# The last output tile of an SSM and SwiGLU kernel: its down projection placed later, and the tile in two column parts

## The chip, the cores and the metric

The kernel runs on one core of a Trainium2 chip. The metric is device time in microseconds (us) of one execution, and each kernel is run several times. A profile is taken of one execution. Every execution also has a span, from its first to its last instruction; in the kernel before it is about 1.8 us less than the device time. Engines are TensorE (PE, its weight loads PEld), VectorE (DVE), ScalarE (ACT), GpSimd (POOL) and the sync engine (SP), which issues most transfers. A name with a q at its end (DVEq, SPq, ACTq) stands for an instruction of that engine's sequencer, such as a semaphore wait or the issue of a transfer; "issue" alone is time in which the engine waited for nothing that the profile shows. The landing of a store is the time from its issue until it is reported as done. A PSUM bank is a piece of the memory that matmuls write to.

## The reference

```python
x  = A_x                                   # (1, 2048, 448) bf16
xn = layernorm(x)
s  = ssm(xn)                               # linear recurrence over 2048 tokens, 448 complex states
g  = silu((silu(xn @ w_gate) * (xn @ w_up)) @ w_down)     # inner width 1792
out = x + s * g                            # (1, 2048, 448) bf16
```

## The kernel before

The 2048 tokens go in four groups of 512, each with four tiles of 128 tokens. For a tile, `down` does the down projection (14 matmuls of 448 columns into one PSUM bank) and ScalarE makes the gate `sg` of it. `out_sum` does the state's output (7 matmuls of 448 columns with `C2`, and 4 small ones that add the skip term), and `finish` multiplies by the gate, adds x and stores. The code is shortened; `...` stands for what is left out.

```python
def down(q, j):
    hd = bank("hd")[:, 0:D]
    for fi in range(NF):                                   # 14
        nc.tensor.matmul(hd, lhsT=Vt_of[q][:, fi, j*P:(j+1)*P], rhs=Wd[:, fi, :], ...)
    sg = work.tile([P, D], BF16, name="sg", bufs=TQ)
    nc.scalar.activation(sg[:], hd, ACT.Silu)
    return sg

def out_sum(q, j):
    y = bank("y")[:, 0:D]
    for n in range(NS):                                    # 7
        h = H_of[q][n // KT][:, n % KT, j*P:(j+1)*P]
        nc.tensor.matmul(y, lhsT=h, rhs=C2[:, n, :], ...)
        if n < KT:                                         # 4: skip term, 128 columns (the last 64)
            ...
    return y

def finish(q, j, y, sg):
    m = q * TQ + j
    t = work.tile([P, D], F32, name="t", bufs=1)
    nc.vector.tensor_tensor(out=t[:], in0=y, in1=sg[:], op=ALU.mult)
    ob = work.tile([P, D], BF16, name="ob")                # two buffers
    nc.vector.tensor_tensor(out=ob[:], in0=t[:], in1=x_all[:, m, :], op=ALU.add)
    nc.sync.dma_start(out=out2d[m*P:(m+1)*P, :], in_=ob[:])

# ... the end of the kernel, the last group of tokens:
q = NQ - 1
bg.finish(q)
sg = [down(q, j) for j in range(TQ)]
for j in range(TQ):
    finish(q, j, out_sum(q, j), sg[j])
```

The instructions stand on each engine in the order in which the program records them.

Of the kernel before, what the change touches and what calls it, by code (L numbers as in the profile page):

```python
# [10 lines left out]
ALU = mybir.AluOpType  # L11
ACT = mybir.ActivationFunctionType
BF16 = mybir.dt.bfloat16
F32 = mybir.dt.float32
# [7 lines left out]
class Background:  # L22
# [16 lines left out]
    def finish(self, owner):  # L39
        while any(step[0] == owner for step in self.steps):  # L40
            self.steps.popleft()[2]()
# [3 lines left out]
def kernel(  # L45
# [17 lines left out]
    nc = tc.nc  # L63
    P = nc.NUM_PARTITIONS
    _, L, D = A_x.shape
    F = B_w_gate.shape[1]
    W = 512
    KF = D // P
    R = D - KF * P
    KT = KF + 1  # L70
    NQ = L // W
    TQ = W // P
    NT = L // P
    NF = F // P
    NS = 2 * KF + 1
# [13 lines left out]
    def blk(k):  # L89
        return slice(k * P, k * P + P) if k < KF else slice(D - P, D)  # L90
# [8 lines left out]
    out2d = out[0]  # L99
# [3 lines left out]
    work = ctx.enter_context(tc.tile_pool(name="work", bufs=2))  # L103
# [3 lines left out]
    def ctile(shape, dtype, name):  # L107
        return const.tile(shape, dtype, name=name)

    def bank(name, dtype=F32):  # L110

        return psum.tile([P, 2048 // mybir.dt.size(dtype)], dtype, name=name, tag="bank")
# [5 lines left out]
    x_all = ctile([P, NT, D], BF16, "x_all")  # L118
    xT = ctile([P, KT, L], BF16, "xT")
# [4 lines left out]
    C2 = ctile([P, NS, D], BF16, "C2")  # L124
    Dd = ctile([P, KT, P], BF16, "Dd")
# [56 lines left out]
    for n in range(2):  # L182
# [11 lines left out]
        out=Id[:], in_=Id[:], compare_op=ALU.not_equal, fill=1.0,  # L194
# [368 lines left out]
    def down(q, j):  # L563

        hd = bank("hd")[:, 0:D]
        for fi in range(NF):
            nc.tensor.matmul(  # L567
                hd, lhsT=Vt_of[q][:, fi, j * P : (j + 1) * P], rhs=Wd[:, fi, :],
                start=(fi == 0), stop=(fi == NF - 1),
            )  # L570
        sg = work.tile([P, D], BF16, name="sg", bufs=TQ)
        nc.scalar.activation(sg[:], hd, ACT.Silu)  # L572
        return sg

    def out_sum(q, j):

        y = bank("y")[:, 0:D]
        m = q * TQ + j
        for n in range(NS):
            h = H_of[q][n // KT][:, n % KT, j * P : (j + 1) * P]  # L580
            nc.tensor.matmul(y, lhsT=h, rhs=C2[:, n, :], start=(n == 0), stop=(n == NS - 1))  # L581
            if n < KT:
                c0 = 0 if n < KF else P - R
                s = blk(n).start
                nc.tensor.matmul(  # L585
                    y[:, s + c0 : s + P], lhsT=xT[:, n, m * P : (m + 1) * P],
                    rhs=Dd[:, n, c0:P], start=False, stop=False,
                )
        return y

    def finish(q, j, y, sg):
        m = q * TQ + j
        t = work.tile([P, D], F32, name="t", bufs=1)
        nc.vector.tensor_tensor(out=t[:], in0=y, in1=sg[:], op=ALU.mult)  # L594
        ob = work.tile([P, D], BF16, name="ob")
        nc.vector.tensor_tensor(out=ob[:], in0=t[:], in1=x_all[:, m, :], op=ALU.add)  # L596
        nc.sync.dma_start(out=out2d[m * P : (m + 1) * P, :], in_=ob[:])


    bg = Background()  # L600
# [82 lines left out]
    for q in range(NQ - 1):  # L683
        sg = []
        for j in range(TQ):
            sg.append(down(q, j))
            bg.run(2.2)
# [3 lines that stand above are left out]
        if q + 2 < NQ:  # L691
            drive(q + 2, "first", 4.0)
            n = (q + 3) * TQ
            last = q + 3 == NQ
            gu(q + 2, bg, 2.2 if last else 1.5, {} if last else {
                0: stats(n, n + 1),
                1: stats(n + 2, n + 3) + sqrt(q + 3),
                2: rstd_of(q + 3) + norms(n, n + 1),
                3: norms(n + 2, n + 3) + transposes(n, n + 1),
                4: transposes(n + 2, n + 3),  # L700
            })
    q = NQ - 1
    bg.finish(q)
    sg = [down(q, j) for j in range(TQ)]
    for j in range(TQ):
        finish(q, j, out_sum(q, j), sg[j])

# [1 line left out]
_INS = ['A_x', 'A_Lambda_re', 'A_Lambda_im', 'A_B_re', 'A_B_im', 'A_C_re', 'A_C_im', 'A_log_dt', 'A_Dskip', 'B_x', 'B_w_gate', 'B_w_up', 'B_w_down']  # L709
_OUTS = [((1, 2048, 448), 'bfloat16')]  # L710
# [25 lines left out]
```

## Time and profile before

| | before |
|---|---|
| device time, median of 3 runs (lowest to highest) | 190.68 us (190.6 to 190.87) |
| span of the profiled execution | 188.8 us |
| TensorE busy | 182.8 us (97%) |
| VectorE busy | 160.0 us (85%) |
| last group: first down projection starts | 167.85 us |
| last matmul's columns are all in ("end of the stream") | 184.53 us |
| last ob ends / last store lands / span ends | 186.07 / 187.8 / 188.8 us |

TensorE is busy from end to end, so the interest lies in the last row: 4.3 us in which it does nothing. The start of the last group stands in the timeline (start us, us, engine, line, what, count):

```profile
167.85 10.76 PE L567 MATMUL hd<-Wd,Vt 128*128 128x448 bf16 x56
```

The 56 are four down projections of 14 matmuls in one run. The end of the stream is the start of the last three matmuls, 183.96, plus three times their spacing of 0.189.

### The profile page before, as it was taken

The page shows a single profiled execution, that of the slowest core. Times are in us where ns is not written, and L with a number is a line of the kernel's source. Part 1 is how long each engine was busy: PE and PEld are TensorE (multiplying, and loading weights), DVE is VectorE, ACT ScalarE, POOL GpSimd, SP SyncE. Part 2 cuts the span into 40 slices and gives each one's busy share as a digit, 9 for nine tenths or more (in the row PEclk, how much of TensorE's full clock was granted, in tenths as well). Part 3 has the DMA queues.
Part 4 walks back from the last instruction along what each step waited for, and adds up shares of the span by engine and source line. Part 5 has one row for each costly group of instructions (what it writes and reads, how often), then busy time and mean ns, then how long its engine had stood idle before and what let it go on. Part 6 is the DMA issues. An engine that isn't in the chain of part 4 may idle for free.

```text
span 188.8 us, 3686 instructions
## 1 busy us (share of the span) xinstructions
PE 182.8 (97%) x1465; PEld 92.5 (49%) x1465; DVE 160.0 (85%) x265; ACT 104.0 (55%) x197; POOL 10.9 (6%) x21
## 2 busy tenths in 40 slices
PE   7899999999999999999999999999999999999991
PEld 3575435555555455544444455544444455555550
DVE  4889995999999999989999899789259999888073
ACT  3288599939998862008987722107987542302200
POOL 6423100000110000000020000000000000000000
PEclk9999999999999999999999999999999999999999
DMA  5999999100012100021006000020000000020011
GB/s 160 343 380 384 377 144 203 28 0 2 0 31 56 31 0 0 0 72 32 0 5 103 6 0 3 24 73 0 3 2 0 3 0 0 0 76 24 0 38 61
DMA packets 20977, 12.59 MB, mean 67 GB/s; under 512 B 10976, under 2 KB 19936, under 8 KB 20960
## 3 DMA queue, kind: packets, MB, share of 16 engines
q1 hardware_dynamic: 20288, 12.10, 24.5%
q10 hardware_dynamic: 544, 0.26, 0.5%
q8 instruction: 11, 0.18, 0.4%
q14 instruction: 6, 0.05, 0.1%
q0 software_dynamic: 128, 0.00, 0.0%
HBM read 8.03 MB, written 1.84 MB: 52 GB/s over the span
## 4 chain that ended last, share of the span: by engine, by line
PE 94%; DVE 2%; DMA 1%; ACT 0%; POOL 0%; issue 0%; DVEq 0%
PE gp L428 24%; PE hd L567 23%; PE up L428 21%; PE y L581 11%; PE pb L428 10%; PE pk L453 2%; PE y L585 2%; DMA x_all<-in_A_x_dram 1%; PE tpb L371 1%; DVE st L230 1%; PE tp L259 1%; DVE t L594 0%; DVE ob L596 0%; ACT xT L261 0%; POOL sd L215 0%; DVE xn L248 0%
## 5 line engine op out<-in xcount | busy, mean ns | idle before, releaser
L428 PE MATMUL gp<-xT,Wg 64*128 64x512 bf16 (+1 forms) x406 | 86.2, 369 | 0.1
L428 PE MATMUL up<-xT,Wu 64*128 64x512 bf16 (+1 forms) x406 | 85.9, 369 | 0.0
L428 PEld LDWEIGHTS <-Wg 64*128 64x128 bf16 x406 | 37.1, 94 | 23.8 <-issue 1.6
L428 PEld LDWEIGHTS <-Wu 64*128 64x128 bf16 x406 | 37.3, 94 | 19.4 <-POOLq L410 0.3
L567 PE MATMUL hd<-Wd,Vt 128*128 128x448 bf16 x224 | 43.0, 353 | 0.0
L554 ACT ACTIVATE gs<-gp 128x512 bf16<-128x512 f32 x56 | 35.0, 626 | 10.9 <-PE gp L428 7.4
L555 ACT ACTIVATE us<-up 128x512 bf16<-128x512 f32 x56 | 35.4, 632 | 0.0
L567 PEld LDWEIGHTS <-Vt 128*128 128x128 bf16 x224 | 21.8, 98 | 21.0 <-issue 0.8
L572 ACT ACTIVATE sg<-hd 128x448 bf16<-128x448 f32 x16 | 8.7, 544 | 33.7 <-PE hd L567 33.7
L559 DVE TENSOR_TENSOR Vt<-gs,us 128x2048 bf16<-128x2048 bf16 (+1 forms) x16 | 17.3, 1082 | 6.3 <-ACT us L555 6.3
L428 PE MATMUL pb<-xT,BT 64*128 64x512 bf16 x168 | 19.2, 376 | 0.0
L594 DVE TENSOR_TENSOR t<-y,sg 128x448 f32<-128x448 f32 x16 | 10.0, 623 | 10.6 <-PE y L581 10.2
L466 ACT ACTIVATE bu_re<-pb 128x512 bf16<-128x512 f32 x12 | 7.3, 609 | 20.9 <-PE pb L428 20.9
L581 PE MATMUL y<-C,H_re 128*128 128x448 bf16 x64 | 17.4, 352 | 0.0
L504 DVE TENSOR_TENSOR_SCAN bu_re<-rcol,H_re,ere 128x512 bf16<-128x512 f32 x12 | 15.1, 1269 | 0.0
L585 PE MATMUL y<-Dd,xT 128*128 128x128 bf16 x64 | 13.6, 212 | 0.0
L428 PEld LDWEIGHTS <-BT 64*128 64x128 bf16 x168 | 8.4, 94 | 10.0 <-issue 1.3
L581 PE MATMUL y<-C,H_im 128*128 128x448 bf16 x48 | 11.7, 353 | 0.0
L504 DVE TENSOR_TENSOR_SCAN bu_im<-rcol,H_im,eim 128x512 bf16<-128x512 f32 x9 | 11.3, 1260 | 0.0
L230 DVE BATCH_NORM_STATS2 st<-x_all 128x6 f32<-128x448 bf16 x16 | 9.8, 615 | 1.5 <-DMA x_all<-in_A_x_dram 1.5
L596 DVE TENSOR_TENSOR ob<-t,x_all 128x448 bf16<-128x448 f32 x16 | 10.0, 625 | 0.5
L215 POOL TENSOR_TENSOR sd<-vep,halves 128x1 bf16<-128x1 bf16 (+1 forms) x7 | 5.7, 814 | 77.2 <-PE up L428 41.8
(95 smaller groups left out, 174.4 us busy)
## 6 DMA issues: line engine op xcount, KB each, us to landing
out_dram<-ob SPq DMA_DIRECT2D x16, 112.0 KB, 1.7
Wd<-in_B_w_down_dram SPq DMA_DIRECT2D x1, 1568.0 KB, 11.8
x_all<-in_A_x_dram SPq DMA_DIRECT2D x1, 896.0 KB, 13.7
Wg<-in_B_w_gate_dram SPq DMA_DIRECT2D x1, 768.0 KB, 7.0
Wu<-in_B_w_up_dram SPq DMA_DIRECT2D x1, 768.0 KB, 8.5
x_all<-in_A_x_dram SPq DMA_DIRECT2D x1, 448.0 KB, 5.2
Wg<-in_B_w_gate_dram SPq DMA_DIRECT2D x1, 384.0 KB, 5.1
Wu<-in_B_w_up_dram SPq DMA_DIRECT2D x1, 384.0 KB, 5.5
```

Of the source, the lines that this page charges most:

```text
L230: nc.vector.bn_stats(out=st[:], in_=x_all[:, n, :])
L428: mm = nc.tensor.matmul(banks[n][i][:, c0:c1], lhsT=weights[n][i][h, d, :], rhs=xT[h, d, q * W + c0 : q * W + c1], start=(first and m == 0 ...
L504: nc.vector.tensor_tensor_scan(out=T["b"][c][:, k, :], data0=rcol[:, k : k + 1].to_broadcast([P, W]), data1=T["e"][c][:, k, :], initial=in ...
L554: nc.scalar.activation(gs[:, i + j, :], gp_[:], ACT.Silu)
L555: nc.scalar.activation(us[:, i + j, :], up_[:], ACT.Copy)
L559: nc.vector.tensor_tensor(out=Vt[:, f0 : f0 + n, :], in0=gs[:, 0:n, :], in1=us[:, 0:n, :], op=ALU.mult)
L567: nc.tensor.matmul(hd, lhsT=Vt_of[q][:, fi, j * P : (j + 1) * P], rhs=Wd[:, fi, :], start=(fi == 0), stop=(fi == NF - 1),)
L572: nc.scalar.activation(sg[:], hd, ACT.Silu)
L581: nc.tensor.matmul(y, lhsT=h, rhs=C2[:, n, :], start=(n == 0), stop=(n == NS - 1))
L585: nc.tensor.matmul(y[:, s + c0 : s + P], lhsT=xT[:, n, m * P : (m + 1) * P], rhs=Dd[:, n, c0:P], start=False, stop=False,)
L594: nc.vector.tensor_tensor(out=t[:], in0=y, in1=sg[:], op=ALU.mult)
L596: nc.vector.tensor_tensor(out=ob[:], in0=t[:], in1=x_all[:, m, :], op=ALU.add)
```

## The change

The intent: shorten what follows the last matmul. The down projection of the last tile goes between the last two output tiles, so that the third tile's VectorE work is over when the last tile comes. The last tile is made in two column parts (256 and 192 columns) with their own PSUM banks, their own buffers (the tags `scr_f` and `scr_a`: scratch of the kernel's beginning, two buffers each) and two queues, so that part one's VectorE work can lie beside part two's matmuls. The diff is shortened.

```diff
-    def out_sum(q, j):
-        y = bank("y")[:, 0:D]
+    def out_sum(q, j, k0=0, k1=KT):
+        y = bank("y")
+        c0, c1 = k0 * P, min(k1 * P, D)
         for n in range(NS):
-            nc.tensor.matmul(y, lhsT=h, rhs=C2[:, n, :], ...)
-            if n < KT:
+            nc.tensor.matmul(y[:, c0:c1], lhsT=h, rhs=C2[:, n, c0:c1], ...)
+            if k0 <= n < k1:
                 ...
-        return y
+        return y[:, c0:c1]

-    def finish(q, j, y, sg):
+    def finish(q, j, y, sg, eng=nc.sync, c0=0, c1=D):
-        t = work.tile([P, D], F32, name="t", bufs=1)
+        of = dict(tag="scr_f") if c1 - c0 < D else dict(bufs=1)
+        t = work.tile([P, c1 - c0], F32, name="t", **of)
         ...
-        ob = work.tile([P, D], BF16, name="ob")
+        of = dict(tag="scr_a") if c1 - c0 < D else {}
+        ob = work.tile([P, c1 - c0], BF16, name="ob", **of)
         ...
-        nc.sync.dma_start(out=out2d[m * P : (m + 1) * P, :], in_=ob[:])
+        eng.dma_start(out=out2d[m * P : (m + 1) * P, c0:c1], in_=ob[:])

-    q = NQ - 1
+    q, last = NQ - 1, TQ - 1
     bg.finish(q)
-    sg = [down(q, j) for j in range(TQ)]
-    for j in range(TQ):
+    sg = [down(q, j) for j in range(last)]
+    for j in range(last):
         finish(q, j, out_sum(q, j), sg[j])
+    sg = down(q, last)
+    for k0, k1, eng in ((0, 2, nc.sync), (2, KT, nc.scalar)):
+        finish(q, last, out_sum(q, last, k0, k1), sg, eng, k0 * P, min(k1 * P, D))
```

More of the change, by code (lines that the diff above doesn't have):

```diff
@@ L573, in down @@
         return sg
-    def out_sum(q, j):
-        y = bank("y")[:, 0:D]
+    def out_sum(q, j, k0=0, k1=KT):
+        y = bank("y")
         m = q * TQ + j
+        c0, c1 = k0 * P, min(k1 * P, D)
         for n in range(NS):
             h = H_of[q][n // KT][:, n % KT, j * P : (j + 1) * P]
-            nc.tensor.matmul(y, lhsT=h, rhs=C2[:, n, :], start=(n == 0), stop=(n == NS - 1))
-            if n < KT:
-                c0 = 0 if n < KF else P - R
+            nc.tensor.matmul(
+                y[:, c0:c1], lhsT=h, rhs=C2[:, n, c0:c1], start=(n == 0), stop=(n == NS - 1)
+            )
+            if k0 <= n < k1:
+                skip = 0 if n < KF else P - R
                 s = blk(n).start
                 nc.tensor.matmul(
-                    y[:, s + c0 : s + P], lhsT=xT[:, n, m * P : (m + 1) * P],
-                    rhs=Dd[:, n, c0:P], start=False, stop=False,
-                )
-        return y
-    def finish(q, j, y, sg):
+                    y[:, s + skip : s + P], lhsT=xT[:, n, m * P : (m + 1) * P],
+                    rhs=Dd[:, n, skip:P], start=False, stop=False,
+                )
+        return y[:, c0:c1]
+    def finish(q, j, y, sg, eng=nc.sync, c0=0, c1=D):
         m = q * TQ + j
-        t = work.tile([P, D], F32, name="t", bufs=1)
-        nc.vector.tensor_tensor(out=t[:], in0=y, in1=sg[:], op=ALU.mult)
-        ob = work.tile([P, D], BF16, name="ob")
-        nc.vector.tensor_tensor(out=ob[:], in0=t[:], in1=x_all[:, m, :], op=ALU.add)
-        nc.sync.dma_start(out=out2d[m * P : (m + 1) * P, :], in_=ob[:])
+        of = dict(tag="scr_f") if c1 - c0 < D else dict(bufs=1)
+        t = work.tile([P, c1 - c0], F32, name="t", **of)
+        nc.vector.tensor_tensor(out=t[:], in0=y, in1=sg[:, c0:c1], op=ALU.mult)
+        of = dict(tag="scr_a") if c1 - c0 < D else {}
+        ob = work.tile([P, c1 - c0], BF16, name="ob", **of)
+        nc.vector.tensor_tensor(out=ob[:], in0=t[:], in1=x_all[:, m, c0:c1], op=ALU.add)
+        eng.dma_start(out=out2d[m * P : (m + 1) * P, c0:c1], in_=ob[:])
     bg = Background()
```

## The prediction

> **What bounds the kernel now.** I read the chain that ended last first, because it says which engine sets the end. The summary of the page gives TensorE (PE) 94% of the span:
>
> ```profile
> PE 94%; DVE 2%; DMA 1%; ACT 0%; POOL 0%; issue 0%; DVEq 0%
> ```
>
> TensorE streams almost without a gap from the first microseconds to 184.5 us, and the change removes no product there. So nearly all of the 188.8 us cannot move; what can is the short stretch after the last matmul. I therefore read the chain again in its last microseconds (start us, us, what):
>
> ```profile
> 184.13 0.58 PE y L581 x3
> 184.71 0.04 DVEq L594
> 184.74 0.04 issue
> 184.79 0.64 DVE t L594
> 185.43 0.02 issue
> 185.45 0.62 DVE ob L596
> ```
>
> The last output tile ends on TensorE, VectorE multiplies it by the gate (t), then adds x (ob), and only then is the result stored. The store's own row, restricted to the last issue, and the program's end (line 731, from the same trace) complete the tail:
>
> ```profile
> L597 SPq DMA_DIRECT2D out_dram<-ob x1: 332/332/332, 186.1 to 186.1; - x1
> DMA to landing us min/median/max: 1.7/1.7/1.7
> ...
> L731 SPq DRAIN  x3: 7/7/13, 188.0 to 188.3; - x3
> ```
>
> So the tail reads: TensorE's stream ends near 184.53 us; t starts at 184.79; ob ends at 185.45 + 0.62 = 186.07; the store is issued at 186.1, lands 1.7 later at about 187.8; about 1.0 us of closing semaphores follows to 188.8. Of these 4.3 us after the stream, only the two VectorE instructions (1.28 us with their gap) are work whose size the change touches; the store's flight and the close are waits. The timeline around the three earlier tiles shows that their VectorE work lies under TensorE's next tile:
>
> ```profile
> 178.65 0.54 ACT L572 ACTIVATE sg<-hd 128x448 bf16<-128x448 f32 x1 [2.10 <-PE hd L567]
> ...
> 181.75 0.62 DVE L594 TENSOR_TENSOR t<-y,sg 128x448 f32<-128x448 f32 x1 [0.23 <-PE y L581]
> ...
> 182.41 0.62 DVE L596 TENSOR_TENSOR ob<-t,x_all 128x448 bf16<-128x448 f32 x1
> ```
>
> VectorE needs 1.28 us for a tile and TensorE 1.52, so VectorE sits idle some 0.23 us before each t.
>
> **What the Trainium skill says, and whether this trace agrees.** "VectorE: DVE Perf Modes", section on the TRN2 errata, gives an fp32 tensor_tensor of N columns (N+151)/0.96 ns. For 448 columns that is 624 ns; the trace has 623 (t) and 625 (ob), and 692 ns for 512 columns where the formula says 691. It agrees, so I use it for the new widths: 256 columns 424 ns, 192 columns 357 ns.
>
> "TensorE: Matmul & The Clock Gate", section "Wait — 56ns, not 53.3ns?", puts back-to-back warm matmuls N/2.4 + about 2.5 ns apart. One output tile is seven of 448 columns, three of 128 and one of 64: 7 x 189.2 + 3 x 55.8 + 29.2 = 1521 ns. In the trace successive tiles start at 178.45, 179.97, 181.49 and 183.01, 1.52 us apart. It agrees.
>
> "DMA: Bandwidth & Descriptors", section "Anatomy of one DMA", says that the fixed part of about 2 us is mostly the wait for the write receipt; its "Specifications" add that pieces under 512 B are below line rate because of a read-modify-write. Here all 16 stores of 112 KB in rows of 896 B have a median landing of 1.7 us. A row of 192 bf16 columns is 384 B, and no store of that row length exists in this trace, so its landing is not settled by it. The same page, "Issuing engines are not separate DMA queues", says a second issuing engine saves only sequencer time; on the before trace the issue on the sync queue costs 0.33 us and is never waited for by the next store.
>
> **The change, part by part.**
>
> *Order.* The fourth down projection (14 matmuls of 448 columns, 14 x 189.2 = 2.65 us) moves from before the first output tile to between the third and the last. TensorE's work is the same. The first output tile then starts 2.65 us sooner, at about 175.8 instead of 178.45. It needs the last H_re, whose VectorE instruction starts at 172.57 and takes 1.23, so it is ready at 173.80: 2.0 us to spare, no stall. What it buys: the third tile's t and ob (0.26 + 1.28 us after its stream) are done under the 2.65 us of down projection, so VectorE is free when the last tile's first part comes. Its own gate has to come in time. The last down projection's stream ends at 183.01 (worked out below); sg starts 0.20 after that as it does now (178.65 against 178.45) and takes 0.54, so it is ready at 183.75. I compare that with the first t below.
>
> *Split on TensorE.* Part one has seven matmuls of 256 columns and two of 128: 7 x 109.2 + 2 x 55.8 = 876 ns. Part two has seven of 192, one of 128 and one of 64: 7 x 82.5 + 55.8 + 29.2 = 662 ns. Sum 1538 against 1521: 7 more matmuls, 0.017 us more. TensorE's stream ends at 184.53 + 0.02 = 184.55; part one at 184.55 - 0.66 = 183.89, and so the last down projection at 183.89 - 0.88 = 183.01. The waits compiled in for the new banks are on events of several microseconds before.
>
> *Split on VectorE.* From the end of a tile's stream to t is 0.26 us now (184.53 to 184.79). So t of part one starts at 183.89 + 0.26 = 184.15, after sg's 183.75; it ends at 184.57. ob of part one runs 184.61 to 185.03, with the same gap of 0.03 to 0.04 between dependent instructions. t of part two could start at 184.55 + 0.26 = 184.81, but VectorE is still in ob. An instruction that does not depend on ob starts before ob's recorded end: at 168.77 + 0.63 = 169.40 an ob ends, and the next instruction has begun at 169.31. So t of part two starts at about 185.03 - 0.09 = 184.94, ends 185.30; ob of part two runs 185.33 to 185.69. Before, ob ended at 186.07. **This is the gain: 0.38 us.** The same from the other side: 1.28 + 0.26 = 1.54 us lay after the stream; now it is 0.26 + 0.13 (waiting for VectorE) + 0.36 + 0.03 + 0.36 = 1.14, less 0.02 for the longer stream.
>
> *Stores.* Part one (64 KB, rows of 512 B) is issued on the sync queue at about 185.06 and lands near 186.8, out of the way. Part two (48 KB) goes out on ScalarE's queue, idle since sg. Its 48 KB instead of 112 KB is at most 0.15 us less by the skill's 436 GB/s (an estimate from that page); the short rows and a queue unused since 1.7 us pull the other way. I set the sum to zero and put it into the range: landing 1.7 after 185.72, at 187.4. The close follows as before.
>
> Span 188.8 - 0.38 = 188.4; time 190.68 - 0.38 = **190.3 us**, 0.2% less.
>
> **The rivals.**
>
> First: the last store eats the gain. 384 B rows are under 512 B, and the two stores are in flight together from 185.72 to 186.8. For it: the page's line on short pieces; both run on the same engines. Against: eight short rows for each of 16 engines are little beside a flight that is mostly receipt, and the first store's data should have moved before the second's starts. If the landing took 0.3 us longer, the time would be 190.6.
>
> Second: short matmuls become bound by the weight loads. Each load is listed with 98 ns, more than the 82.5 ns spacing of part two. Were that the spacing, part two would be some 7 x 15 = 0.11 us longer, and since VectorE is busy for 0.13 us of that anyway nothing much would be seen at the end (190.3 still). Against it: the trace already has whole 128-row loads at a shorter spacing:
>
> ```profile
> 9.70 1.06 PE L371 MATMUL tpb<-Id,nat 128*128 128x128 bf16 x16
> ```
>
> Sixteen in 1.06 us, a load each: (1.06 - 0.22) / 15 = 0.056 us apart.
>
> Third: the order hurts: TensorE waits for H_re, or the first t waits for sg. The margins above, 2.0 and 0.4 us, speak against it; a wait of 0.3 for sg would pass on only in part, giving 190.5.
>
> Fourth: the store lands sooner, being smaller, by up to 0.15 us: 190.15.
>
> **Range and chances.** The VectorE sum is from measured durations and good to about 0.1 us. The landing is good to 0.2 us in either direction. The three runs before spread over 0.27 us (190.6 to 190.87), so a median can be off by 0.1. Together about 0.25 to each side, a little more to the slow side for the store: 190.05 to 190.65. A change of 2% would be 3.8 us; the whole tail is 4.3 us and no new wait of that size is in sight, so within 2% is near certain.
>
> **What would show it right or wrong.** In the profile after: the first output tile on TensorE at about 175.8 with no gap before it; y to y spacing of 0.109 and 0.082 us for the new widths; t and ob of 424 and 357 ns; t of part two beginning about 0.4 us after TensorE's stream ends, held by VectorE and not by TensorE; last ob near 185.7; last issue on ScalarE's queue, landing 1.7 us later; span 188.4. I am wrong if the last landing takes clearly more or less than 1.7 us, if the first t waits for ScalarE, or if TensorE's stream ends more than 0.1 us from 184.55.

## The result, and the profile after

The changed kernel took 190.31 us (median of 4 runs, 190.14 to 190.72) against 190.64 for the kernel before (4 runs, 190.6 to 190.87). A ratio here is the mean time of one kernel's fast runs over that of the other's, so not quite the ratio of the medians. It was 0.9983, with an interval of 0.9965 to 1.0001. Two later sets of five and six runs gave 190.15 and 190.20, with ratios of 0.9973 and 0.9976 (told below).

The first thing to see in the profile after is that its span is 188.9 us, longer than before. This one execution was the slowest of its four, at 190.72. The timelines of VectorE near the beginning show why. The first fence is before, the second after (in brackets: idle time before the instruction, and what ended it):

```profile
3.77 0.62 DVE L230 BATCH_NORM_STATS2 st<-x_all 128x6 f32<-128x448 bf16 x1
```

```profile
4.38 0.63 DVE L230 BATCH_NORM_STATS2 st<-x_all 128x6 f32<-128x448 bf16 x1 [0.48 <-DMA x_all<-in_A_x_dram]
...
168.46 8.11 PE L567 MATMUL hd<-Wd,Vt 128*128 128x448 bf16 x42
```

The second tile of x landed late in that execution, its statistics began 0.61 us later, and the last group began 0.61 us later too (168.46 against 167.85). The change touches nothing there. The two delays go together in other profiles too: of the thirteen profiles besides that of before, eleven have the same delay against it, to 0.02 us, at these statistics and at the last group (e4's and e8's groups lost another 0.17 and 0.22 in between). A span read without this would say that nothing was gained. From the start of the last group, the tail of the timeline after reads so:

```profile
173.17 1.22 DVE L498 TENSOR_TENSOR H_re<-H_re,tmp 128x2048 bf16<-128x2048 bf16 x1
...
176.22 0.10 PEld L582 LDWEIGHTS <-H_re 128*128 128x128 bf16 x1
...
183.62 0.27 PE L582 MATMUL y<-C,H_re 128*128 128x256 bf16 x1
...
183.82 0.54 ACT L572 ACTIVATE sg<-hd 128x448 bf16<-128x448 f32 x1 [6.67 <-PE hd L567]
...
184.91 0.41 PE L582 MATMUL y<-C,H_im 128*128 128x192 bf16 x3
```

H_re is ready at 174.39, 1.8 us before the first output tile's first weight load (176.22) and 2.0 before its first matmul (176.41), so the new order costs TensorE nothing. Part one starts on TensorE at 183.62. The gate is ready at 184.36. The last stream ends at 184.91 + 3 x 0.0825 = 185.16, which is 16.70 us after the group's start; before it was 16.68. The chain of waits then shows what lies after the stream (start us, us, what):

```profile
184.70 0.02 DVEq L598
184.72 0.04 issue
184.76 0.43 DVE t L598
185.20 0.02 issue
185.22 0.42 DVE ob L601
185.65 0.28 DVE t L598
185.92 0.02 issue
185.95 0.36 DVE ob L601
```

Four VectorE instructions stand in a row where there were two, but the first two lie beside part two's matmuls. The second t is on the chain behind ob of part one, and not behind a matmul: VectorE held it. (The chain cuts the overlap of neighbours; the timeline has this t starting at 185.56.) The last ob ends at 186.31, 17.85 us after the group's start, against 18.22 before. The last store:

```profile
L602 ACTq DMA_DIRECT2D out_dram<-ob x1: 353/353/353, 186.3 to 186.3; - x1
...
DMA to landing us min/median/max: 1.5/1.5/1.6
```

It landed 1.5 us after its issue instead of 1.7. From the group's start the span ends at 20.4 us, before at 20.95: some 0.5 us gained, of which 0.37 is VectorE's and about 0.2 the store's, each rounded. A little of it is lost again outside the span: device time exceeds the span by 1.82 to 1.88 us in the four executions of the changed kernel (spans are known to 0.1), by about 1.79 in the mean of the kernel before.

### The profile page after: what moved, and what is told of

It reads as the page before. It is cut to its first block, busy times and chain, and to the rows that moved or that the text cites. A ratio compares the mean times of both kernels' runs of the same rounds, so it can differ in the third digit from the quotient of the medians.

```text
span 188.9 us, 3703 instructions
## 1 busy us (share of the span) xinstructions
PE 182.9 (97%) x1472; PEld 93.0 (49%) x1472; DVE 160.3 (85%) x267; ACT 104.0 (55%) x197; POOL 10.9 (6%) x21
## 4 chain that ended last, share of the span: by engine, by line
PE 94%; DMA 2%; DVE 2%; ACT 0%; POOL 0%; issue 0%; SPq 0%; DVEq 0%
PE gp L428 24%; PE hd L567 23%; PE up L428 21%; PE y L582 11%; PE pb L428 10%; PE pk L453 2%; DMA x_all<-in_A_x_dram 2%; PE y L588 2%; PE tpb L371 1%; PE tp L259 1%; DVE ob L601 0%; DVE t L598 0%; DVE st L230 0%; ACT xT L261 0%; POOL sd L215 0%
## 5 line engine op out<-in xcount | busy, mean ns | idle before, releaser
L598 DVE TENSOR_TENSOR t<-y,sg 128x448 f32<-128x448 f32 (+2 forms) x17 | 10.1, 595 | 10.0 <-PE y L582 9.6
L582 PE MATMUL y<-C,H_re 128*128 128x448 bf16 (+2 forms) x68 | 17.6, 342 | 0.0
L582 PE MATMUL y<-C,H_im 128*128 128x448 bf16 (+2 forms) x51 | 11.9, 342 | 0.0
L601 DVE TENSOR_TENSOR ob<-t,x_all 128x448 bf16<-128x448 f32 (+2 forms) x17 | 10.2, 597 | 0.6
```

Source lines behind the costliest of these rows:

```text
L582: nc.tensor.matmul(y[:, c0:c1], lhsT=h, rhs=C2[:, n, c0:c1], start=(n == 0), stop=(n == NS - 1))
L598: nc.vector.tensor_tensor(out=t[:], in0=y, in1=sg[:, c0:c1], op=ALU.mult)
```

## The experiments

Twelve runs were made. The kernel before was measured beside them, but not anew for each: e1 to e4 share its 11 executions, e5 to e8 share 9, and e9 to e12 are compared with the same 9 and one more. "ob" and "span" are the ends of the last ob and of the span, counted from the start of the last group; spans are known to 0.1.

| run | ob | span | last store: KB, landing | device time: median (lowest to highest) | ratio to before (interval) |
|---|---|---|---|---|---|
| before | 18.22 | 20.95 | 112, 1.7 | 190.65 beside e1 to e4, 190.81 and 190.80 beside the others | |
| e1_again | 17.84 | 20.4 | 48, 1.5 | 190.15 (190.07 to 190.26) | 0.9973 (0.9961 to 0.9984) |
| e2_order_only | 18.21 | 20.95 | 112, 1.7 | 190.84 (190.59 to 191.5) | 1.0012 (0.9999 to 1.0025) |
| e3_split_only | 18.15 | 20.7 | 48, 1.5 | 190.64 (190.43 to 190.88) | 1.0 (0.9987 to 1.0013) |
| e4_one_queue | 17.85 | 20.3 | 48, 1.5 | 190.12 (190.06 to 190.4) | 0.9973 (0.9961 to 0.9985) |
| e5_wide_last | 17.78 | 20.3 | 64, 1.6 | 190.13 (190.1 to 190.4) | 0.997 (0.9958 to 0.9983) |
| e6_narrow_last | 18.28 | 20.8 | 16, 1.4 | 190.52 (190.49 to 190.88) | 0.999 (0.9977 to 1.0002) |
| e7_t_bf16 | 17.61 | 20.2 | 48, 1.5 | 190.17 (189.87 to 190.23) | 0.9962 (0.995 to 0.9975) |
| e8_shared | 18.03 | 20.55 | 48, 1.5 | 190.83 (190.72 to 190.87) | 1.0 (0.9986 to 1.0014) |
| e9_again | 17.85 | 20.4 | 48, 1.5 | 190.20 (190.11 to 190.91) | 0.9976 (0.9962 to 0.9991) |
| e10_t_bf16 | 17.62 | 20.2 | 48, 1.5 | 189.94 (189.85 to 190.14) | 0.9954 (0.9941 to 0.9968) |
| e11_shared | 18.03 | 20.55 | 48, 1.5 | 190.64 (190.59 to 191.35) | 1.0 (0.9986 to 1.0014) |
| e12_shared_t | 18.03 | 20.6 | 48, 1.5 | 190.49 (190.43 to 190.75) | 0.9987 (0.9973 to 1.0001) |

e1 to e4 ran together on one chip, e5 to e8 together and e9 to e12 together on another. All results were correct.

**e1_again: the changed kernel, unaltered.**

> The changed kernel again, unaltered, to have its time on the chip and in the rounds of the other runs. All runs are also read from the first matmul of the last group of down projections (167.85 us in the profile of before, 168.46 after), which leaves out how early the loads at the start came. From there: last ob ends 17.85 us later (before 18.22), span ends 20.4 later (before 20.95). Theory (the VectorE work after the last stream is shorter by 0.37 and the smaller store lands 0.15 sooner): 0.45 to 0.5 us faster than before in time, about 190.2. Rival (the 0.33 of the first measurement is all there is, and the tail only looks shorter): 190.3 to 190.4.

It came as the theory said: 190.15. None of its five spans was over 188.4, where the first set had 188.9 and 188.5 among its four. By the ratio the gain is 0.27% of 190.7, 0.5 us, which is what the tail shows less the 0.06 or so that is lost outside the span. e9_again, a third set, agrees:

> The changed kernel once more, as the measure for the three runs beside it: last ob 17.85 us after the group's start, 190.1 to 190.2.

It gave 190.20, with one execution of 190.91.

**e2_order_only: the move without the split.**

```diff
-    for k0, k1, eng in ((0, 2, nc.sync), (2, KT, nc.scalar)):
-        finish(q, last, out_sum(q, last, k0, k1), sg, eng, k0 * P, min(k1 * P, D))
+    finish(q, last, out_sum(q, last), sg)
```

> Down projection of the last tile moved as in the change, the last output tile whole on the sync queue. Theory (the move alone only makes VectorE free earlier, which a whole last tile has no use for): the last ob ends 18.2 us after the group's start, as before; time 190.6, the same as before. Rival (the move is what gains): 17.85 and 190.3.

The last ob ended at 18.21, as before, and the two lowest of its six runs are 190.59, as before. The other four scatter up to 191.5; I cannot say why; only an execution of 190.59 was profiled, and nothing in its tail differs. So the move alone gains nothing: VectorE is free earlier, and a whole last tile gives it nothing to do earlier.

**e3_split_only: the split without the move.**

```diff
-    sg = [down(q, j) for j in range(last)]
+    sg = [down(q, j) for j in range(TQ)]
     ...
-    sg = down(q, last)
+    sg = sg[last]
```

> Last tile in two parts, four down projections first as before. Theory: the third tile's t and ob now stand in the way. From the group's start the last stream ends at 16.70, the third tile's ob at 16.70, t of part one starts at 16.61, its ob ends at 17.49, t of part two starts at 17.40 and the last ob ends at 18.15: only 0.07 better than before; with the smaller store's 0.15 the time is 190.4 to 190.5. Rival (the split is what gains, the move is not needed): 17.85 and 190.2.

The last ob ended at 18.15, to the hundredth as worked out. The chain shows the third tile in the way:

```profile
184.14 0.18 DVE ob L601
184.32 0.36 issue
184.68 0.43 DVE t L598
```

The ob that starts at 184.14 is the third tile's, of 0.63 us in the timeline. Part one's stream had ended at 184.10 (the last stream at 184.51 + 3 x 0.0825 = 184.76, less 0.66 for part two), so its t could have begun at 184.37, 0.27 after as usual, but VectorE was not free and it began at 184.68. The expected time of 190.4 to 190.5 was missed: the median is 190.64, and only the lowest run is at 190.43. The profiled execution began its last group 0.22 later than the profile of before (168.07), which is as much as its tail had gained; of the other four there is no trace, so the miss is not explained by this. Together e2 and e3 are the main lesson: at the last ob the move gains 0.01, the split 0.07, and both together 0.37, because each removes what would hold the other.

**e4_one_queue: both parts stored from the sync queue.**

```diff
-    for k0, k1, eng in ((0, 2, nc.sync), (2, KT, nc.scalar)):
+    for k0, k1, eng in ((0, 2, nc.sync), (2, KT, nc.sync)):
```

> As after, but both parts are stored from the sync queue. Theory (the first issue of 0.33 us is over 0.3 us before the second is due, and the landing depends on the size of the store): last ob at 17.85 after the group's start, last issue at once, landing 1.5 us, same time as after within 0.05. Rival (the idle queue is what made the landing 1.5 instead of 1.7): landing 1.7 and 0.15 to 0.2 us slower than after.

The theory held: same tail, same time, and the second store lands in 1.5 us from this queue too. The second queue of the change does no work. So the 0.2 us by which the last landing became shorter (1.7 before, 1.5 after) is not the queue's.

How the landing goes with the size can be read from the list of transfers. The first three lines are the last three stores of e3, the fourth is e6's last (told below):

```profile
out_dram<-ob SPq DMA_DIRECT2D x1, 112.0 KB, 1.7
out_dram<-ob SPq DMA_DIRECT2D x1, 64.0 KB, 1.6
out_dram<-ob ACTq DMA_DIRECT2D x1, 48.0 KB, 1.5
...
out_dram<-ob ACTq DMA_DIRECT2D x1, 16.0 KB, 1.4
```

**e5_wide_last: 192 columns first, 256 last.**

```diff
-    for k0, k1, eng in ((0, 2, nc.sync), (2, KT, nc.scalar)):
+    for k0, k1, eng in ((2, KT, nc.sync), (0, 2, nc.scalar)):
```

> As after, but the narrow part (192 columns) first on the sync queue and the wide one (256) last on ScalarE's queue. Theory (VectorE is free before the last stream ends, so the last t waits for TensorE and not for VectorE, but is itself longer by 2 x 67 ns): t of part two starts 0.26 us after the last stream, last ob ends 17.84 us after the group's start, as after; the 64 KB store lands in 1.6: time as after or 0.1 slower, 190.15 to 190.25. Rival (the 0.13 us for which VectorE held t of part two is lost time, to be had by freeing it): last ob at 17.71 and 190.0.

The wait changed hands: t of part two is now released by the matmul.

```profile
184.20 0.56 PE y L582 x5
184.76 0.02 issue
184.79 0.44 DVE t L598
```

But it started sooner than I had expected. The stream ended at 184.26 + 3 x 0.109 = 184.59 (184.26 is the start of its last three matmuls), so this t began 0.20 after it and not 0.26. The lines of before and of after show the difference: there a "DVEq" entry and its "issue" stand ahead of a first t, here not. The first t of a tile waits for TensorE and for ScalarE, this one for TensorE alone. The count bears this out: in the profile after and in e5 there are 17 instructions t and 16 such events, in e8, e11 and e12, where part two has to wait for more, 17. So I put the 0.06 down to the second wait; a part two that is released by the matmul was seen in this one profile only. If so, in the changed kernel VectorE holds t of part two not for the 0.13 of my prediction but for 0.40 - 0.20 = 0.20. The last ob ended at 17.78, between theory (17.84) and rival (17.71). The 0.07 gained was used up by the larger store, 1.6 instead of 1.5, and the time is the same as e1's.

**e6_narrow_last: 384 columns first, 64 last.**

```diff
-    for k0, k1, eng in ((0, 2, nc.sync), (2, KT, nc.scalar)):
+    for k0, k1, eng in ((0, 3, nc.sync), (3, KT, nc.scalar)):
```

> As after, but parts of 384 and 64 columns. Theory (part one's t and ob of 1.15 us cannot lie under a part two of 0.23 us on TensorE): t of part two starts about 0.85 us after the last stream, last ob ends 18.27 us after the group's start, 0.05 later than before; the 16 KB store lands in 1.4 to 1.5, so the time is 190.4 to 190.5, most of the gain lost. If the matmuls of 64 columns cannot go 0.029 us apart but are held by their weight loads to 0.056, the last stream ends 0.2 later and the last ob stays at 18.27. Rival (what counts is only how little is left after the last stream): last ob at about 17.45 and 189.7.

The last ob ended at 18.28 against an expected 18.27, and the time of 190.52 is only just outside the 190.4 to 190.5. A very small last part is not better: part one's VectorE work of 1.15 us then comes after the stream. The same trace settles the prediction's second rival. Four matmuls of 64 columns, each with its own load of 128 rows, stand in the timeline of TensorE:

```profile
184.38 0.28 PE L582 MATMUL y<-C,H_re 128*128 128x64 bf16 x4
```

One takes 0.193, so they are (0.28 - 0.19) / 3 = 0.03 us apart, though each load is listed with 98 ns. Loads do not bound the spacing here, down to 64 columns.

**e7_t_bf16 and e10_t_bf16: t of the two parts in bf16.**

```diff
-        t = work.tile([P, c1 - c0], F32, name="t", **of)
+        t = work.tile([P, c1 - c0], F32 if c1 - c0 == D else BF16, name="t", **of)
```

> As after, but t of the two parts is bf16 (the whole tiles keep fp32), so that ob has only 16-bit operands. Theory (the gain is the VectorE time after the last stream, nothing else): ob of 256 columns takes 0.29 us instead of 0.42, ob of 192 columns 0.26 instead of 0.36, t of part two starts at 0.26 instead of 0.40 after the last stream, last ob ends 17.60 us after the group's start, 0.24 sooner than after: 189.9. Rival (past this point something else sets the end, the store of part one or the close): less than 0.1 of it reaches the time, 190.1.

> The version with bf16 t for the two parts, beside the changed kernel on the same chip. Theory: last ob at 17.61, as in its first run, and 0.2 to 0.25 us less than the changed kernel in the means of five runs. Rival (its first run's 190.17 shows no gain over 190.15): within 0.1 of it.

With only 16-bit operands ob becomes shorter. The chain of e10:

```profile
184.43 0.44 DVE t L598
184.86 0.02 issue
184.88 0.29 DVE ob L601
185.18 0.28 DVE t L598
185.46 0.02 issue
185.48 0.26 DVE ob L601
```

The last ob ended at 17.61 and 17.62, against an expected 17.60. In the first run the time looked like a miss (190.17, where 189.9 was expected), with two executions at 189.87 and three near 190.2; one of the three is the profiled one, which began its last group at 168.23, 0.2 later than e1's. Run beside the changed kernel, it took 189.94 against 190.20, 0.26 less. This version beats both kernels, by 0.46% over the one before, at the price of one more rounding to bf16.

**e8_shared and e11_shared: the parts use the buffers of whole tiles.**

```diff
-        t = work.tile([P, c1 - c0], F32, name="t", **of)
+        t = work.tile([P, D], F32, name="t", bufs=1)[:, 0 : c1 - c0]
         ...
-        ob = work.tile([P, c1 - c0], BF16, name="ob", **of)
+        ob = work.tile([P, D], BF16, name="ob")[:, 0 : c1 - c0]
```

> As after, but the two parts use the one t buffer and the two ob buffers of the whole tiles. Theory (t of part two must not overwrite t of part one before its ob has read it, so it now waits for that ob's end and its event): t of part two starts 0.03 after the ob of part one ends instead of 0.09 before, last ob ends at 17.96, 0.12 later than after: 190.3. The ob buffers' stores have landed more than 1 us before. Rival (own buffers make no difference as VectorE runs in order anyway): 17.84 and 190.15.

> Shared buffers again, because its first run was 0.68 us slower than the changed kernel while its tail was only 0.18 longer (last ob at 18.03) and its time exceeded its span by 2.17 us against 1.8 to 1.9 in the others. Theory (that excess belongs to that run and not to the kernel): last ob at 18.03, time 0.2 slower than the changed kernel, 190.3 to 190.4. Rival (sharing costs something that the tail does not show): again 0.5 to 0.7 slower, 190.8.

The chain of e11 where part two follows part one:

```profile
184.80 0.43 DVE ob L599
185.23 0.03 issue
185.26 0.02 DVEq L597
185.28 0.04 issue
185.32 0.37 DVE t L597
```

t of part two must wait for ob of part one to have read the one t buffer. It starts 0.10 after that ob's end (185.22 in the timeline), where with its own buffer it starts 0.09 before. I had expected 0.03 after, the gap between t and its own ob; the separate event ahead of a t is the difference. So the own buffers are worth 0.18 us at the last ob, half of VectorE's gain.

The time, however, was 0.63 us (e8) and 0.44 us (e11) worse than e9's on the same chip. Neither number of e11's expectation was met, 190.64 lying between 190.3 to 190.4 and 190.8, but the rival is right that the excess belongs to the kernel: in all ten executions the device time exceeds the span by 2.10 to 2.19 us, against 1.81 to 1.91 in all executions of the kernels with own buffers. These 0.28 us and the 0.18 at the last ob are together about the 0.44 between e11 and e9. The excess lies outside what the profile records.

**e12_shared_t: only t is shared.**

```diff
-        t = work.tile([P, c1 - c0], F32, name="t", **of)
+        t = work.tile([P, D], F32, name="t", bufs=1)[:, 0 : c1 - c0]
```

> Only t is shared, ob has its own buffers. Theory (the wait of t of part two for the ob of part one is the whole cost of sharing): last ob at 18.03, same time as with both shared. Rival (the ob buffers and their waits on stores cost part of it): last ob at 17.85 to 17.95, and nearer the changed kernel.

In the tail the theory holds: the last ob ends at 18.03 with or without a shared ob. The time is 190.49, 0.15 below e11's where the same was expected, but the intervals of the two ratios overlap. Its excess over the span is 1.97 to 2.11 in its four executions, so the shared t alone brings more than half of the 0.28. What makes up the excess outside the span stays open.

## Why the prediction was right or wrong

That the first median, 190.31, met the predicted 190.3 so closely was luck: two of its four executions (190.72 and 190.38) lay above every one of e1's. The later sets put the time at 190.15 to 190.20 and the gain at 0.5 us, not 0.38. Step by step:

- **Order: right.** No gap on TensorE, 2.0 us to spare for H_re before the first matmul (2.0 predicted), and the gate ready 0.40 us before the first t (0.40 predicted). e2 shows that this step alone gains nothing.
- **Split on TensorE: right.** The stream ended 0.02 later, at 16.70 after the group's start instead of 16.68.
- **Split on VectorE: right in the sum.** Predicted from the end of the stream: t of part two at 0.39 and the last ob at 1.14; measured 0.40 and 1.15. The gain at the last ob was 0.37 against 0.38, and e3, e6 and e7 came within 0.01 of sums worked out in the same way. Two terms were mis-sized: e5 was 0.06 sooner than its sum and e8 0.07 later, each, as read above, by an event ahead of a t that was wrongly counted in or left out. In the prediction the first of them did not show: a t that waits for the stream alone starts 0.20 after it and not 0.26 (e5, one profile), so VectorE's hold was 0.20 and not 0.13, and the start at 0.40 is the same.
- **Stores: the step that failed.** The prediction said "I set the sum to zero and put it into the range: landing 1.7". The landing was 1.5, in all ten profiles whose last store had 48 KB, and this is the missing 0.1 to 0.2 us; a landing clearly off 1.7 was on the prediction's own list of signs of being wrong. The mechanism that was to cancel the smaller size was not seen: the idle queue cost nothing (e4), and the landing fell with the size of the store, 1.7, 1.6, 1.5 and 1.4 us for 112, 64, 48 and 16 KB (a first part of 64 KB in e4 took 1.5), while the rows became shorter too. Size and row length changed together here, so a small cost of short rows could be hidden in it; one large enough to undo the smaller size is ruled out.
- **Rivals.** The fourth (a smaller store lands sooner, 190.15) is what happened. The first is refuted by the landings, the second by e6, the third by the two margins above.
- **What hid the error.** The first four executions had a mean of 190.37, with one of 190.72. Its profile shows the cause, the second tile of x landing 0.6 us late; of the other three there is no trace. That scatter is larger than the term in question; only counting from the last group's start told them apart.

## What to carry to other kernels

The end of a kernel is a chain of its own: last matmul, elementwise work, store, close. Splitting its last tile pays only if the elementwise engine is free when the first part comes, so split and order belong together (0.37 us at the last ob together, 0.07 and 0.01 alone), and the parts should be sized so that part one's elementwise work ends about when part two's data is there, neither much smaller nor larger. Three parts, or e5's sizes together with t in bf16, were not tried. When a gain is smaller than the scatter of the start, measure from a late common point in the trace, and give the parts their own buffers, since a wait on the same engine cost more here than the order alone (0.18 us at the last ob).

## What the Trainium skill lacked or had wrong

- "DMA: Bandwidth & Descriptors", section "Anatomy of one DMA", gives a fixed part of about 2.0 us with a term in size, fitted for transfers issued from GpSimd, and has no such figures for stores from the sync or ScalarE queue. Here their whole landing was 1.7 us at 112 KB, 1.5 to 1.6 at 64, 1.5 at 48 and 1.4 at 16. The loss that the page names for pieces under 512 B was not visible in stores this small: rows of 384 B and of 128 B are the last two of these four.
- "TensorE: Matmul & The Clock Gate", section "Back-to-back issue gap", calls about 81 ns the sustained spacing of a load and a matmul of 128 columns, and N/2.4 + 2.5 the isolated one. Here sixteen loads with transposes of 128 columns went 0.056 us apart and loads with matmuls of 64 columns 0.03; the second formula held for the 56 of 448 columns, 0.189 us apart.
- No page gives the cost of a second wait of one VectorE instruction: a t that waits for TensorE and ScalarE began 0.26 to 0.27 us after the stream, one that by my reading waits for TensorE alone 0.20 (one profile).
- "VectorE: DVE Perf Modes", section "The DRAIN you can't avoid", found in a row of eight copies that a semaphore after each costs nothing extra. Here a wait on its own engine did cost: t of part two began 0.09 us before the end of the ob ahead of it without a wait for it, 0.10 after with one.
